# A linear-attention and feed-forward kernel on one Trainium2 core: one padded bf16 copy of v in place of two copies, and a new written order of the work

## The chip, the cores and the metric

The kernel runs on one core of one Trainium2 chip (trn2). The time is device microseconds (us) of one launch; the median of three runs of the kernel before is 179.17 us (178.84 to 181.43). All profiles show the one core. Engines are named as in the profile: PE is TensorE's matrix multiply and PEld its loading of weights, DVE is VectorE, ACT is ScalarE, POOL is GpSimd, SP is SyncE, which issues all DMAs here.

## The reference

A gated recurrence over time (4 batches, 8 heads, 768 steps, head size 48) is followed by a feed-forward layer over the 3072 tokens:

```
f = 1.0 / (1.0 + np.exp(-f_logit))
for t in range(S):
    state = f[:, :, t, :, None] * state + np.einsum('bhd,bhe->bhde', k[:, :, t], v[:, :, t])
    y[:, :, t] = np.einsum('bhd,bhde->bhe', q[:, :, t], state)
x = y.transpose(0, 2, 1, 3).reshape(B * S, H * D)      # 3072 x 384
h = x @ w_in                                           # 384 -> 2048
out = np.maximum(0.01 * h, h) @ w_out                  # 2048 -> 384
```

Inputs and output are fp32; the kernel's matrix products take bf16 operands and add up in fp32.

## The kernel before, in words

**Chunks and units.** Time is cut into six chunks of 128 steps. Within a chunk, the recurrence becomes matrix products: scores of k and q, masked to the lower triangle, times v, plus the state at the chunk's start times q. The work is cut into 12 units of 256 tokens. Units 0 to 3 ("paired") hold chunks 0 and 1 of one batch each; units 4 to 11 hold one chunk of two batches each. Words in the written order have the form name_unit_part, with the PSUM banks behind an @; a last number 0 or 1 picks an engine where there is a choice (for SBUF work 0 is DVE and 1 is POOL; where PSUM is read 0 is DVE and 1 is ACT).

**Steps of a unit.** The loads Lf, Lk, Lq, Lv (line 201 for paired units, 205 for others) bring 192 KB each. ACT works out log f (ge, gl; lines 233 and 245). PE sums it along time (cs, lines 254 to 265) with the constant matrices bu, bs and ut and the vector half_ones; ACT takes exponentials of the sums (dec, lines 273 to 279: em, at, end). DVE or POOL multiplies k and q with them (k, q, line 285). The products are turned: by PE and a copy out of PSUM for units 0 to 3 (tk, tq, line 319; ck, cq, lines 332 and 334), by a DMA that SP issues for the others (xk, xq, line 339). PE makes scores (sc, lines 355 and 362), DVE masks them (mk, lines 372 and 376; units 0 to 3 use the constant pair_mask, which eight small DVE copies of bu and bs build, Mp, line 139). PE multiplies masked scores with v (mx, line 393) and adds the state's part (within mx, and ms for paired units, the same line). DVE or ACT copies the result to xT (xt, lines 453 and 455). The state is carried by PE (pt, lines 466 and 471: k times v), DVE (sf, lines 481 and 483) and POOL (sb, lines 488 and 491).

**Feed-forward.** For each unit, eight up words (line 499) of six matmuls each multiply xT with w_in; ACT applies the leaky ReLU (pr, line 504); eight dn words (line 520) of four matmuls each, four for each half of the unit, multiply with w_out; DVE or ACT copies out (ob, lines 529 and 531) and SP stores (st, line 535). The very last half of unit 11 is done in two column halves (dc, oc, sh; lines 542 to 557). The weights arrive in fp32 (WI, WO, lines 154 and 158) and are cast by DVE, POOL or ACT (ci, co, lines 165 and 167); an up word of a group needs that group's ci.

**The copies of v.** mx multiplies in blocks of 32 output columns, three to a pair of heads (a pair has 2 x 48 = 96 columns). Blocks 0 and 2 lie within one head. Block 1 straddles: its first 16 columns are the end of head 0 and the next 16 the beginning of head 1, and each head's masked scores are multiplied separately, so each head needs 32 columns of which the other head's 16 are zero. So v is kept twice: vb holds v in bf16 (line 291), and v2 holds four groups of 16 columns a pair, the outer two copied from v (lines 297 and 300) and the inner two zero (cleared once, line 108). Paired units take three casts a half (one at line 291, two at 297), others two a unit (291 and 300).

**What sets the order.** The schedule is written out by hand: the string order (lines 576 to 642) is read word by word, and each engine gets its instructions in that order. Every engine runs its own queue strictly in order, and an instruction that waits holds up all behind it on that engine. SP's queue holds the loads, the DMA transposes and the stores. F words (line 97) are matmuls of zeros on PE whose result is not used. At the start the order holds the clearing of pads (Zl, Zk, Zq, Zv, lines 104 and 108), of the state buffers (Zb, line 111), and the building of constants on POOL (Mt: ut; Ms: bs; Mu: bu; both of the latter line 118; Mh: half_ones; Mi: ident).

## Time and profile before

| What | Value |
|---|---|
| Median of three runs | 179.17 us (178.84 to 181.43) |
| The profiled execution's own time | 178.92 us |
| Its span in the trace | 177.1 us, granted TensorE clock 0.999 |
| PE matmul busy | 170.0 us, 2308 instructions |
| PE weight loads busy | 124.9 us |
| DVE busy | 80.2 us |
| ACT busy | 108.8 us |
| POOL busy | 77.3 us |
| DMA | 34.45 MB, mean 194 GB/s |

The span is measured from the first to the last instruction of the program that the trace holds; the execution's own time is 1.8 us longer. The views used are: the page (shares of engines and of the chain that ended last), the windows (busy time of each engine in stretches of the span), the waits (who waited for whom), the chain in order of time, the timeline of an engine, and the groups of instructions by line and shape. In a timeline row stand the start, the length, the engine, the line, the operation, output<-inputs, shapes and count; a bracket at the end gives the idle time before it and what ended it.

### The profile page before, as it was taken

The numbers are of one execution on the slowest core, as the hardware profiler recorded it, in microseconds if no ns is written. First come the engines' busy times: TensorE is split into PE (matmuls) and PEld (weight loads), VectorE is DVE, ScalarE is ACT, GpSimd is POOL, SyncE is SP. The second block draws the span as 40 slices with busy tenths as digits, with TensorE's granted clock in tenths as the row PEclk, the third lists the DMA queues.
The fourth block names the chain that finished last, engine by engine and source line by source line (L and its number), as shares of the span: only waits on it lengthen the run. The fifth ranks groups of instructions, "written<-read, shape, count | busy, mean of one in ns | idle before, by whom it ended". The sixth has DMA issues, their size and how long they took to land.

```text
span 177.1 us, 5587 instructions
## 1 busy us (share of the span) xinstructions
PE 170.0 (96%) x2308; PEld 124.9 (71%) x2310; DVE 80.2 (45%) x170; ACT 108.8 (61%) x230; POOL 77.3 (44%) x141
## 2 busy tenths in 40 slices
...
GB/s 127 270 286 331 343 314 367 381 288 238 213 156 78 187 176 250 180 222 182 219 188 211 228 163 166 196 195 225 192 184 209 141 232 167 48 44 0 4 67 113
DMA packets 108330, 34.45 MB, mean 194 GB/s; under 512 B 101008, under 2 KB 107280, under 8 KB 108304
## 3 DMA queue, kind: packets, MB, share of 16 engines
...
q8 instruction: 18, 0.29, 0.7%
...
## 4 chain that ended last, share of the span: by engine, by line
PE 87%; DVE 4%; DMA 3%; ACT 2%; issue 2%; POOL 1%; SPq 1%; DVEq 0%; POOLq 0%
PE ps L520 34%; PE ps L499 34%; PE ps L393 6%; DMA f_raw<-in_f_logit_dram 3%; PE ps L362 2%; PE ps L319 2%; DVE wm L372 2%; PE ps L262 2%; PE ps L542 1%; PE ps L355 1%; PE ps L471 1%; PE ps L97 1%; DVE kh L285 1%; POOL sb L491 1%; DVE sf L481 1%
## 5 line engine op out<-in xcount | busy, mean ns | idle before, releaser
L504 ACT ACTIVATE gT<-ps 128x512 bf16<-128x512 f32 x96 | 53.1, 608 | 27.1 <-PE ps L499 26.7
L499 PE MATMUL ps<-xT,w_in 128*128 128x256 bf16 x576 | 69.6, 273 | 0.1
L520 PE MATMUL ps<-w_out,gT 128*128 128x384 bf16 x368 | 67.3, 326 | 0.0
L499 PEld LDWEIGHTS <-w_in 128*128 128x128 bf16 x576 | 55.1, 98 | 9.2 <-DVE xT L455 0.4
L520 PEld LDWEIGHTS <-gT 128*128 128x128 bf16 x368 | 34.4, 98 | 19.8
L285 POOL TENSOR_TENSOR qh<-q_raw,at 128x768 bf16<-128x768 f32 (+1 forms) x13 | 18.3, 1405 | 21.9 <-ACT end L279 7.3
L376 DVE TENSOR_TENSOR wm<-ps,ut 128x512 bf16<-128x512 f32 x32 | 20.1, 684 | 10.6 <-PE ps L362 10.6
L273 ACT ACTIVATE em<-ps 128x384 bf16<-128x384 f32 x24 | 11.9, 496 | 19.8 <-PE ps L265 9.3
L483 DVE TENSOR_TENSOR sf<-sf,ps 64x192 f32<-64x192 f32 x32 | 11.2, 349 | 18.0 <-PE ps L471 16.1
L491 POOL CAST sb<-sf 64x192 bf16<-64x192 f32 x40 | 14.5, 362 | 7.2 <-DVE sf L481 4.9
L285 POOL TENSOR_TENSOR kh<-k_raw,em 128x768 bf16<-128x768 f32 (+1 forms) x9 | 14.4, 1604 | 5.7 <-DMA q_raw<-in_q_dram 3.2
L291 POOL CAST vb<-v_raw 128x384 bf16<-128x384 f32 (+1 forms) x13 | 8.5, 650 | 16.7 <-DMA v_raw<-in_v_dram 13.3
L488 POOL TENSOR_TENSOR sf<-sf,end 128x192 f32<-128x192 f32 x16 | 8.9, 554 | 14.2 <-DVE sf L483 13.9
L531 DVE COPY osb<-ps 128x384 f32<-128x384 f32 x13 | 7.2, 554 | 16.1 <-PE ps L520 10.5
L233 ACT ACTIVATE e<-f_raw 128x384 f32<-128x384 f32 (+1 forms) x16 | 11.1, 695 | 2.3 <-DMA f_raw<-in_f_logit_dram 2.3
L274 ACT ACTIVATE at<-ps 128x384 bf16<-128x384 f32 x24 | 11.9, 497 | 0.0
L372 DVE TENSOR_TENSOR wm<-ps,pair_mask 128x512 bf16<-128x512 f32 x16 | 10.4, 687 | 3.3 <-PE ps L355 3.0
L245 ACT ACTIVATE lf<-e 128x384 bf16<-128x384 f32 (+1 forms) x16 | 10.9, 683 | 0.3
L455 DVE CAST xT<-ps 128x384 bf16<-128x384 f32 x11 | 6.1, 566 | 10.3 <-PE ps L393 10.0
L453 ACT CAST xT<-ps 128x384 bf16<-128x384 f32 x13 | 6.6, 527 | 5.3 <-PE ps L393 5.0
L529 ACT COPY osb<-ps 128x384 f32<-128x384 f32 x10 | 4.9, 493 | 6.9 <-PE ps L520 6.9
L97 PE MATMUL ps<-zeros 128*128 128x512 bf16 x20 | 7.8, 467 | 1.4 <-DVE zeros L93 1.2
...
## 6 DMA issues: line engine op xcount, KB each, us to landing
...
```

Source lines behind the costliest of these rows:

```text
L233: nc.scalar.activation(e[:, part], src[:, part], AF.Exp, scale=-1.0)
L245: nc.scalar.activation(dst, src, AF.Ln, bias=1.0)
L273: nc.scalar.activation(ems[j % 2][:, a], t[:, 0:H * D], AF.Exp, scale=1.0)
L274: nc.scalar.activation(ats[j % 2][:, a], t[:, 0:H * D], AF.Exp, scale=-1.0)
L285: eng.tensor_mul(heads(j, to[j % NR], a)[:, :, :, 0:D], raw_heads(j, x, a), decays(j, by, a))
L372: nc.vector.tensor_mul(w.rearrange("t (s p) n -> t s p n", s=2), src.rearrange("t (s p n) -> t s p n", s=2, p=2), pair_mask[:, :, None, :] ...
L376: nc.vector.tensor_mul(w, src.rearrange("t (p n) -> t p n", p=P2), ut[:, None, :].to_broadcast([128, P2, 128]))
L483: nc.vector.tensor_add(sf[rows], sf[rows], new)
L491: nc.gpsimd.tensor_copy(out=sb[rows, :, y * D:y * D + D], in_=sf[rows])
L499: nc.tensor.matmul(pm[:, i, :], w_in_of(ff, kk), xT_of(j)[:, kk].rearrange("t a s -> t (a s)"), start=(kk == 0), stop=(kk == NK - 1))
L504: nc.scalar.activation(gT_of(j)[:, 2 * g:2 * g + 2, :], pm, AF.Prelu, alpha=0.01)
L520: nc.tensor.matmul(po, gT_of(j)[:, ff, 128 * a:128 * a + 128], w_out_b[ff // 2][:, ff % 2, :], start=(ff == 0), stop=(ff == NF - 1))
```

## The change

Three things change.

First, v has one bf16 copy instead of two. vbs becomes a tile of 80 columns a head: 48 of v and 32 of padding. In a pair of heads the columns are head 0 (0 to 47), zeros (48 to 79), head 1 (80 to 127), and padding that nothing reads (128 to 159). Blocks 0 and 2 of a pair are columns 0 to 31 and 96 to 127; the straddling block's two parts are columns 32 to 63 (the end of head 0, then 16 zeros) and 64 to 95 (16 zeros, then the beginning of head 1). So cast_v is one cast a call in place of two or three, the tiles v2 are gone, clear_v clears columns 48 to 79 of each pair (as many elements as clear_v2 cleared), and mix and state read from the one tile.

Second, the written order is another one. It holds the same words the same number of times, except that the F words hold 25 matmuls of zeros in place of 22. Within it, engines change for some words: the v casts of units 0 to 3 go 3 to DVE and 5 to POOL (before 1 and 7), those of units 4 to 11 go 6 to DVE and 2 to POOL (before 2 and 6); the k products of units 0 to 3 go 5 and 3 (before 7 and 1); xt goes 16 to DVE and 8 to ACT (before 11 and 13); of the casts of w_out DVE has 3 and POOL 3 (before 5 and 1); five of the eight Zb, and Mi, stand in POOL's queue ahead of Mu, where none of them did.

Third, the banks of PSUM behind the @ are new too, as part of the order.

The diff, with the two orders up to ms_2 and the new one's end:

```diff
--- before.py
+++ after.py
@@ -66,8 +66,8 @@
     ems = tiles(2, [128, 2, H * D], BF16, "em")
     ats = tiles(2, [128, 2, H * D], BF16, "at")
     ends = tiles(4, [128, 2, P2], FP32, "end")
-    vbs = tiles(3, [128, 2, H, D], BF16, "vb")
-    v2s = tiles(3, [128, 2 * P2, 4, 16], BF16, "v2")
+    VW = D + 32
+    vbs = tiles(3, [128, 2, H, VW], BF16, "vb")
     kTs = tiles(2, [128, 2 * P2, 128], BF16, "kT")
     qTs = tiles(2, [128, 2 * P2, 128], BF16, "qT")
     wms = tiles(8, [128, 4, 128], BF16, "wm")
@@ -104,8 +104,12 @@
             engine(e).memset(ts[i][:, :, :, D:64], 0.0)
         return go
 
-    def clear_v2(i, e):
-        engine(e).memset(v2s[i][:, :, 1:3, :], 0.0)
+    def clear_v(i, e):
+        engine(e).memset(pairs_of_v(vbs[i])[:, :, D:VW], 0.0)
+
+    def pairs_of_v(t):
+
+        return t.rearrange("t a (p j) n -> t (a p) (j n)", j=2)
 
     def clear_state(b, i, e):
         engine(e).memset(sbs[b][i], 0.0)
@@ -286,20 +290,7 @@
         return go
 
     def cast_v(j, a, e):
-        vb, v2 = vbs[j % 3], v2s[j % 3]
-        eng = engine(e)
-        eng.tensor_copy(out=heads(j, vb, a), in_=raw_heads(j, "v", a))
-        if paired(j):
-            p = slice(0, P2) if a == 2 else slice(2 * a, 2 * a + 2)
-            src = by_pair(raw(j, "v")).rearrange("t (p j) s d -> t j s p d", j=2)
-            dst = v2.rearrange("t (s p) n e -> t n s p e", s=2)
-            for i in range(2):
-                eng.tensor_copy(out=dst[:, 3 * i, :, p], in_=src[:, i, :, p, 32 - 32 * i:48 - 32 * i])
-        else:
-            a2 = slice(a, a + 1) if a < 2 else slice(0, 2)
-            eng.tensor_copy(out=v2[:, P2 * a2.start:P2 * a2.stop, 0:4:3, :],
-                                  in_=raw(j, "v")[:, a2].rearrange("t a (p j) d -> t (a p) (j d)", j=2)[:, :, 32:64]
-                                  .rearrange("t p (j e) -> t p j e", j=2))
+        engine(e).tensor_copy(out=heads(j, vbs[j % 3], a)[:, :, :, 0:D], in_=raw_heads(j, "v", a))
 
     def turned(j, x):
         return (kTs if x == "k" else qTs)[j % 2]
@@ -398,7 +389,7 @@
 
         for i, b in enumerate(bank):
             st[j]["py", i] = b
-        vb, v2 = vbs[j % 3], v2s[j % 3]
+        vp = pairs_of_v(vbs[j % 3])
         jobs = []
         if paired(j):
             halves = range(2) if a == 2 else (a,)
@@ -413,10 +404,8 @@
                 for g, which, p, y in todo:
                     for i in range(2):
                         rows = slice(64 * i, 64 * i + 64)
-                        if which == "v":
-                            lhsT = vb[rows, s, 2 * p + y, 16 * y:16 * y + 32]
-                        else:
-                            lhsT = v2[rows, P2 * s + p, 2 * y:2 * y + 2, :]
+                        at = 96 * y if which == "v" else 32 + 32 * y
+                        lhsT = vp[rows, P2 * s + p, at:at + 32]
                         jobs.append((i, g, lhsT, wm_of(j, p // 2, y)[rows, 2 * s + p % 2, :]))
             accumulate(j, jobs, (0,) if a else ())
             return
@@ -427,9 +416,9 @@
         for i in range(2):
             for y in range(2):
                 for p in range(P2):
-                    jobs.append((i, 3 * p + 2 * y, vb[:, i, 2 * p + y, 16 * y:16 * y + 32], wm_of(j, i, y)[:, p, :]))
+                    jobs.append((i, 3 * p + 2 * y, vp[:, P2 * i + p, 96 * y:96 * y + 32], wm_of(j, i, y)[:, p, :]))
                 for p in range(P2):
-                    jobs.append((i, 3 * p + 1, v2[:, P2 * i + p, 2 * y:2 * y + 2, :], wm_of(j, i, y)[:, p, :]))
+                    jobs.append((i, 3 * p + 1, vp[:, P2 * i + p, 32 + 32 * y:64 + 32 * y], wm_of(j, i, y)[:, p, :]))
         accumulate(j, jobs, (0, 1))
 
     def mix_state(j):
@@ -464,12 +453,12 @@
                     for i in range(2):
                         rows = slice(64 * i, 64 * i + 64)
                         nc.tensor.matmul(banks[bank[i]][:, 96 * p:96 * p + 96], kh[rows, s, 2 * p:2 * p + 2, :],
-                                         vb[rows, s, 2 * p:2 * p + 2, :], start=(s == 0), stop=(s == 1))
+                                         vb[rows, s, 2 * p:2 * p + 2, 0:D], start=(s == 0), stop=(s == 1))
             return
         st[j]["pt", a] = bank[0]
         for p in range(P2):
             nc.tensor.matmul(banks[bank[0]][:, 96 * p:96 * p + 96], kh[:, a, 2 * p:2 * p + 2, :],
-                             vb[:, a, 2 * p:2 * p + 2, :], start=True, stop=True)
+                             vb[:, a, 2 * p:2 * p + 2, 0:D], start=True, stop=True)
 
     def state_add(j, a):
         sf = sfs[batch(j, a)]
@@ -565,7 +554,7 @@
         "dc": down_cols, "oc": out_cols, "sh": store_cols,
         "Lf": load("f"), "Lk": load("k"), "Lq": load("q"), "Lv": load("v"),
         "WI": load_w_in, "WO": load_w_out, "ci": cast_w(w_in_b, 0), "co": cast_w(w_out_b, 8),
-        "Zl": clear_pad(lfs), "Zk": clear_pad(khs), "Zq": clear_pad(qhs), "Zv": clear_v2, "Zb": clear_state,
+        "Zl": clear_pad(lfs), "Zk": clear_pad(khs), "Zq": clear_pad(qhs), "Zv": clear_v, "Zb": clear_state,
         "Mu": make_block(bu, mybir.AluOpType.is_gt), "Ms": make_block(bs, mybir.AluOpType.is_ge), "Mi": make_ident,
         "Mo": make_ones, "Mh": make_half_ones, "Mp": make_pair_mask, "Zz": clear_zeros, "F": fill, "Mt": make_ut,
     }
@@ -573,73 +562,73 @@
 
 
     order = """
-    Zz F_7_512@7 Lf_1_0 Mt Ms Zb_0_0_0 Zl_2_0 Zv_1_1 Lf_0_1 Zl_1_0 Zv_0_1 Zb_0_1_0 Zk_0_0 Zb_1_1_0 Lf_0_0 Zq_0_0
-    Zq_1_0 Lk_0_1 Mh Mu Mp_0 Zk_2_1 Lq_0_1 Zb_1_0_0 Zl_0_0 Lq_0_0 Lk_0_0 ge_1_0 Lk_1_0 Zk_1_1 gl_1_0 ge_0_1
-    Zb_3_0_1 Zq_2_1 Mo Lq_1_0 gl_0_1 Mi Lf_1_1 Lv_0_1 ge_0_0 gl_0_0 cs_1_0@0 Zb_2_0_0 Lv_0_0 cs_0_1@1 F_2_512@7
-    dec_0_1 cs_0_0@2 F_1_512@7 Lk_1_1 dec_0_0 k_0_1_0 tk_0_1@3 q_0_1_0 tq_0_1@4 F_1_512@2 Zb_2_1_1 Lq_1_1
-    k_0_0_0 dec_1_0 Lv_1_1 ck_0_1_1 Lv_1_0 cq_0_1_0 tk_0_0@5 F_1_512@4 q_1_0_0 q_0_0_1 tq_0_0@6 Zv_2_0 Lf_2_1
-    cq_0_0_1 WI_5 k_1_0_1 ck_0_0_0 sc_0_1@7.1 ge_1_1 Lf_2_0 tq_1_0@2 gl_1_1 mk_0_1_1 sc_0_0@4.0 mk_0_0_1
-    mk_0_0_0 cq_1_0_1 tk_1_0@3 cs_1_1@5 F_3_512@0 ck_1_0_0 sc_1_0@6.1 v_0_1_1 v_0_0_1 pt_0_2@0.2 F_1_512@3
-    mk_0_1_0 WI_1 WI_0 dec_1_1 Lq_2_1 k_1_1_0 tk_1_1@4 q_1_1_1 WI_2 sf_0_0 v_1_0_1 tq_1_1@3 cq_1_1_1 ge_2_1
-    gl_2_1 ck_1_1_0 Lk_2_1 mx_0_2@5.7 xt_0_0_1 sb_0_0 v_1_1_1 WI_4 sc_1_1@0.4 F_3_512@3 mk_1_0_1 ci_5_1 mk_1_1_1
-    ms_0 xt_0_1_1 cs_2_1@3 mk_1_0_0 Lq_2_0 pt_1_2@1.4 F_1_512@6 sf_1_0 sb_1_0 up_0_5@5 F_1_512@1 mk_1_1_0 Lk_2_0
-    mx_1_2@6.7 ge_2_0 gl_2_0 dec_2_1 pr_0_5 ms_1 cs_2_0@1 ci_1_0 xt_1_1_0 WI_3 Lv_2_0 WI_7 xt_1_0_1 up_0_1@0
-    ci_0_1 Lv_2_1 q_2_1_1 up_1_5@3 pr_1_5 Zb_3_1_1 up_0_0@7 up_1_1@5 ci_2_0 sf_0_1 tq_2_1@6 up_1_0@3 pr_0_1 WO_0
-    k_2_1_0 up_0_2@0 WO_1 dec_2_0 tk_2_1@2 pr_0_2 pr_0_0 ci_4_0 sb_0_1 pr_1_1 cq_2_1_0 k_2_0_0 up_1_2@1 q_2_0_1
-    pr_1_2 up_0_4@0 up_1_4@6 Lf_3_0 WI_6 sf_1_1 pr_1_4 ci_3_0 tq_2_0@7 sb_1_1 tk_2_0@5 F_1_512@4 cq_2_0_1
-    ck_2_0_0 up_1_3@1 WO_2 sc_2_0@4.6 Lk_3_0 ck_2_1_0 v_2_0_1 pr_1_0 WO_3 mk_2_0_1 ci_7_2 mk_2_0_0 sc_2_1@5.7
-    up_0_3@2 pr_0_3 WO_7 mk_2_1_1 v_2_1_1 pt_2_2@3.6 pr_1_3 up_0_7@4 Lf_3_1 mk_2_1_0 up_1_7@2 pr_0_7 sf_2_0
-    sb_2_0 co_0_2 pr_1_7 ge_3_0 co_1_0 mx_2_2@7.1 xt_2_0_0 ms_2 xt_2_1_1 dn_0_0_0@5 ci_6_1 dn_0_1_0@4 sf_2_1
...
+    Zz F_10_512@7 Lf_0_1 Lf_1_0 Lf_0_0 Lk_0_1 Lk_0_0 Zb_1_1_0 Lq_0_1 Zb_1_0_1 Mi Zq_2_0 Zl_1_1 Lq_0_0 Zv_2_0
+    Zk_2_0 Zq_0_0 Mt Lv_0_0 Ms Zq_1_1 Lv_0_1 Zv_0_0 Lq_1_0 Lf_1_1 Zb_2_1_1 Lk_1_0 Zb_3_1_1 Mh Zk_0_1 Lq_1_1
+    Zb_0_0_1 Zl_0_0 Lk_1_1 Zb_0_1_1 Mu Mp_0 Zk_1_1 Zb_2_0_1 Lf_2_1 ge_0_1 gl_0_1 Lv_1_1 ge_1_0 gl_1_0 cs_0_1@0
+    F_1_512@7 Lv_1_0 Zb_3_0_0 Lf_2_0 WI_5 WI_1 ge_0_0 gl_0_0 cs_0_0@1 WI_0 cs_1_0@2 dec_0_1 k_0_1_0 tk_0_1@3
+    F_1_512@7 WI_4 Zv_1_1 dec_0_0 k_0_0_0 q_0_0_0 q_0_1_1 tq_0_1@4 cq_0_1_0 dec_1_0 v_0_0_1 ck_0_1_0 tk_0_0@5
+    ck_0_0_1 Lk_2_0 Lq_2_1 tq_0_0@6 F_1_512@1 cq_0_0_0 WI_2 WI_3 v_0_1_1 pt_0_2@7.0 sf_0_0 sc_0_1@1.2 mk_0_1_1
+    sc_0_0@4.3 F_3_512@6 mk_0_0_1 mk_0_0_0 ge_1_1 gl_1_1 cs_1_1@5 dec_1_1 q_1_0_1 tq_1_0@6 cq_1_0_0 k_1_0_1
+    tk_1_0@7 F_5_512@2 ck_1_0_1 sc_1_0@2.3 Lq_2_0 Mo k_1_1_0 tk_1_1@4 q_1_1_1 tq_1_1@6 sb_0_0 mk_0_1_0
+    mx_0_2@5.7 ms_0 Zl_2_0 v_1_0_1 mk_1_0_1 mk_1_0_0 ck_1_1_1 cq_1_1_1 sc_1_1@1.4 mk_1_1_1 mk_1_1_0 xt_0_1_1
+    Lk_2_1 v_1_1_1 pt_1_2@3.6 F_4_512@2 mx_1_2@2.7 sf_1_0 ge_2_0 gl_2_0 cs_2_0@4 sb_1_0 xt_0_0_0 ge_2_1 gl_2_1
+    cs_2_1@1 dec_2_1 ci_5_1 sf_0_1 xt_1_0_1 up_0_5@3 ci_1_0 up_0_1@5 pr_0_1 pr_0_5 ci_0_0 up_0_0@0 pr_0_0 WI_7
+    WO_0 sb_0_1 ms_1 sf_1_1 WO_1 ci_4_0 up_0_4@1 pr_0_4 xt_1_1_0 up_1_5@2 up_1_1@6 up_1_4@5 Lv_2_1 Lv_2_0
+    dec_2_0 WI_6 pr_1_5 k_2_0_0 tk_2_0@3 pr_1_4 up_1_0@0 pr_1_0 ci_2_0 up_0_2@7 pr_0_2 q_2_0_0 ck_2_0_0 q_2_1_1
+    tq_2_1@1 cq_2_1_0 WO_2 up_1_2@4 tq_2_0@2 cq_2_0_1 pr_1_2 ci_3_1 WO_3 up_1_3@5 pr_1_3 k_2_1_1 tk_2_1@0
+    ck_2_1_0 co_0_2 Lf_4_1 Lf_4_0 WO_5 pr_1_1 up_0_3@7 pr_0_3 sc_2_0@3.1 mk_2_0_0 mk_2_0_1 Lf_3_0 Lf_3_1
+    sc_2_1@2.4 mk_2_1_1 mk_2_1_0 ci_7_1 up_1_7@0 up_0_7@5 pr_0_7 pr_1_7 v_2_1_0 co_1_1 dn_0_1_0@3 dn_1_0_0@6
+    dn_1_1_0@1 v_2_0_0 pt_2_2@7.4 sf_2_0 sb_1_1 WO_4 mx_2_2@5.2 WO_7 Lk_3_1 ci_6_2 up_1_6@0 sb_2_0 ms_2 xt_2_1_0
...
+    dc_11_1_0_2 dc_11_1_0_3 oc_11_1_0_1 sh_11_1_0
```

99 lines of the change are left out of this document (49 added, 50 removed).

## The prediction

> **What bounds the kernel now.** I read the page's shares first, then the windows, then PE's waits, then PE's chain.
>
> ```profile
> PE 170.0 (96%) x2308; PEld 124.9 (71%) x2310; DVE 80.2 (45%) x170; ACT 108.8 (61%) x230; POOL 77.3 (44%) x141
> ...
> PE 87%; DVE 4%; DMA 3%; ACT 2%; issue 2%; POOL 1%; SPq 1%; DVEq 0%; POOLq 0%
> ```
>
> The second line is the chain that ended last: 87% of the span is PE itself. The windows (span stretch, length, then busy us of PE, PEld, DVE, ACT, POOL, granted clock, DMA share, GB/s) say where the rest lies:
>
> ```profile
> 0.00:22.00 22.00, 18.64 (x354) 11.09 (x357) 17.40 (x44) 15.63 (x36) 15.21 (x47) 1.00 0.96 271
> 22.00:60.00 38.00, 37.69 (x503) 28.27 (x499) 21.93 (x46) 26.09 (x56) 17.12 (x31) 1.00 0.92 249
> 60.00:174.00 114.00, 113.72 (x1489) 85.57 (x1462) 40.88 (x81) 66.94 (x140) 45.00 (x65) 1.00 0.78 164
> 174.00:177.10 3.10, 0.00 (x0) 0.00 (x0) 0.00 (x0) 0.10 (x1) 0.00 (x0) 0.95 0.27 98
> ```
>
> From 22 us to 174 us PE is idle for 0.31 + 0.28 us in all. The last 3.1 us are the last copy and store. So three places remain where an order can win or lose: the first 22 us, in which PE has only 354 of its 2308 matmuls and DVE is the fullest engine after PE (17.40 of 22); the 0.6 us of holes; and new holes that the order might make in a stretch that has none. PE's own waits (us in total, times, longest), the chain's rows (start, length, what) and PE's timeline give the holes a name:
>
> ```profile
> PE ps L393 <- POOL sb L491: 0.3, 1, 0.3
> ...
> PE ps L97 <- issue: 0.2, 1, 0.2
> ```
>
> ```profile
> 22.09 2.64 PE ps L499 x24
> ...
> 33.50 0.68 POOL sb L491
> ...
> 173.78 0.32 ACT osb L550
> ```
>
> ```profile
> 33.72 0.23 PE L393 MATMUL ps<-qT,sb 128*32 128x128 bf16 x1
> 34.22 0.35 PE L393 MATMUL ps<-qT,sb 128*32 128x128 bf16 x11 [0.27 <-POOL sb L491]
> ```
>
> At 22.09 the dense stream begins: 24 matmuls in 2.64 us, so an up word is 0.66 us. The one later wait of PE that the list names is ms_2 for the state copy sb_2_0, which ends at 34.18; PE started nothing from 33.72 to 34.22. PE waited only 0.2 us for "issue" anywhere, which is what an instruction block that comes late would look like: an order that minds TensorE's blocks has next to nothing to win back there.
>
> **The change, part by part.** *The casts.* The groups by line and shape (busy us, mean ns of one | idle before):
>
> ```profile
> L291 POOL CAST vb<-v_raw 128x768 bf16<-128x768 f32 x6 | 4.9, 823 | 9.9 <-DMA v_raw<-in_v_dram 6.7 <-PE ps L265 3.2
> L297 POOL CAST v<-v_raw 128x64 bf16<-128x64 f32 x14 | 3.5, 280 | 0.0
> L291 POOL CAST vb<-v_raw 128x384 bf16<-128x384 f32 x7 | 3.5, 503 | 6.7 <-DMA v_raw<-in_v_dram 6.6
> L300 POOL CAST v<-v_raw 128x256 bf16<-128x256 f32 x6 | 2.4, 398 | 0.0
> ...
> L291 DVE CAST vb<-v_raw 128x768 bf16<-128x768 f32 x2 | 1.2, 618 | 2.8 <-DMA v_raw<-in_v_dram 2.8
> ...
> L291 DVE CAST vb<-v_raw 128x384 bf16<-128x384 f32 x1 | 0.3, 349 | 0.0
> ```
>
> POOL loses the small casts (3.5 + 2.4 us) and keeps 5 x 0.503 + 2 x 0.823 = 4.2 us of the 8.4; together 10.1 us fewer. DVE goes from 1.6 us of large casts to 3 x 0.349 + 6 x 0.618 = 4.8 us. The rows hold no cast into rows of 80 columns; it may cost as now (349 ns for 384 elements) or as much as a two-input product of that size (560 ns, row 7.82 below), so 4.8 to 8 us; I take 4.8, since the number of elements is what the rows follow. None of it is on PE's chain: POOL is idle 100 us of the span, DVE 97 us, and PE waits for no v in the list above. Value: 0, with a bound of 0.5 us for a cast on DVE that stands among the four masks of one unit (v_6 stands between the third and the fourth). If DVE's slack after 60 us (40.88 busy of 114) were gone, each such cast would cost its 0.62 us.
>
> *PE's own work.* The words are the same, so the matmuls are the same and their operands have the same shapes. The F words go from 22 to 25 matmuls, all ahead of the dense stream, where PE waits anyway: 0.
>
> *The constants.* Five state clears and the identity now stand ahead of bu on POOL. POOL's timeline at the start:
>
> ```profile
> 0.73 0.20 POOL masks.py:65 MEMSET ut<- 128x128 bf16 x1 [0.29 <-POOLq L662]
> ...
> 3.94 0.57 POOL L104 MEMSET kh<- 128x256 bf16 x2
> 4.44 0.43 POOL L111 MEMSET sb<- 128x384 bf16 x1
> 4.80 0.32 POOL L104 MEMSET qh<- 128x256 bf16 x1
> ...
> 5.63 0.45 POOL L111 MEMSET sb<- 128x384 bf16 x1
> ```
>
> bu was ready at 3.94. From 0.73 to 5.63 (4.90 us) POOL did ut, bs, half_ones, bu, the identity, five pads and one state buffer. The new queue up to bu has three pads instead of five (two take from 3.94 to 4.44, so 0.50 less) and five state buffers instead of one (4 x 0.36 more, from 4.44 to 4.80): bu is ready at about 0.73 + 4.90 - 0.50 + 1.44 = 6.6 us, 2.6 us later. What hides that is ACT:
>
> ```profile
> 4.59 0.32 PE L254 MATMUL ps<-lf,bu 128*128 128x192 bf16 x1 [0.24 <-ACT lf L245]
> ...
> 6.33 0.52 ACT L233 ACTIVATE e<-f_raw 128x384 f32<-128x384 f32 x1 [0.82 <-DMA f_raw<-in_f_logit_dram]
> ...
> 7.32 0.47 ACT L273 ACTIVATE em<-ps 128x384 bf16<-128x384 f32 x1
> ```
>
> The first sum on PE moves from 4.59 to 6.6, but in both orders ACT's first exponential of a sum stands behind the third gate (ge_0_0, gl_0_0), whose load lands at 6.3, so em comes at 7.3 either way. Were that cover gone, the delay would be 2.0 us. What is late next is pair_mask, eight DVE copies that wait for bu, and behind them on DVE the first k product (7.82 below).
>
> *The start, by DVE's queue.* The rows that price it:
>
> ```profile
> 7.82 0.56 DVE L285 TENSOR_TENSOR kh<-k_raw,em 128x384 bf16<-128x384 f32 x1 [1.02 <-ACT em L273]
> ...
> 11.02 2.10 DVE L372 TENSOR_TENSOR wm<-ps,pair_mask 128x512 bf16<-128x512 f32 x3
> 13.04 0.41 DVE L334 COPY kT<-ps 128x512 bf16<-128x512 bf16 x1
> ...
> 13.96 1.19 DVE L285 TENSOR_TENSOR kh<-k_raw,em 128x384 bf16<-128x384 f32 x1
> ...
> 19.02 0.74 DVE L481 TENSOR_TENSOR sf<-ps,end 64x192 f32<-64x192 f32 x2 [0.76 <-ACT e L233]
> ...
> 20.40 1.14 DVE L167 CAST w_in<-k_raw 128x768 bf16<-128x768 f32 x1
> ```
>
> ```profile
> 13.83 0.91 POOL L285 TENSOR_TENSOR qh<-q_raw,at 128x384 bf16<-128x384 f32 x1 [0.83 <-ACT end L276]
> ...
> 19.44 0.81 POOL L491 CAST sb<-sf 64x192 bf16<-64x192 f32 x2 [1.15 <-DVE sf L481]
> 20.31 0.82 POOL L167 CAST w_in<-f_raw 128x768 bf16<-128x768 f32 x1
> ```
>
> DVE's new queue, from em at 7.8 to the last mask of unit 1: k, k, q and later k_1_1 (4 x 0.56), four copies out of the turning (4 x 0.41), sf_0_0 (0.74), eight masks (8 x 0.70): 10.2 us, so mk_1_1_0 ends at 18.0 if DVE never waits. Then sf_1_0 to 18.75, on POOL sb_1_0 to 19.6 and behind it ci_5_1 to 20.4, and the first up word at 20.4; each of the next three up words needs a cast of w_in from DVE's queue (ci_1, ci_0, ci_4, with 2 x 0.74 of state and 0.57 of xt before and between). From 18.75: 0.57 + 0.74, then ci_1 and ci_0, 0.74, then ci_4. Other DVE casts of this shape took 0.56:
>
> ```profile
> L167 DVE CAST w_out<-q_raw 128x768 bf16<-128x768 f32 x2 | 1.1, 560 | 0.1
> ```
>
> With such casts the fourth up word ends at 23.1, with casts of 1.14 at 24.9. In the old order one up word stands ahead of 22.09 and three follow, so the fourth ends at 22.09 + 3 x 0.66 = 24.07, with the same other words behind it. So the start is worth -0.9 to +0.8; the middle is zero. DVE's queue can also meet POOL on the way: k_1_1 took 1.19 us at 13.96 instead of 0.56 while POOL ran its q product from 13.83 to 14.74, so a meeting costs up to 0.63, and the new order puts q_0_1 on POOL just as DVE starts k_0_1. I add half of one meeting: **+0.3** (bounds -0.9 and +1.4).
>
> [...]
>
> *The hole at ms_2.* In the new order the word up_1_6 (0.66 us) stands between mx_2 and ms_2, so sb_2_0 has that much longer; the hole from 33.72 to 34.22 goes: **-0.5**. What is late next is nothing on PE; dn words follow.
>
> *New holes.* Between mx and a unit's first up word PE needs other work for the copies xt:
>
> ```profile
> L455 DVE CAST xT<-ps 128x384 bf16<-128x384 f32 x11 | 6.1, 566 | 10.3 <-PE ps L393 10.0
> ```
>
> Units 5, 6, 8 and 11 now have both copies on DVE (2 x 0.57 = 1.13 and the wait for PSUM) behind two dn words or their like (1.3 us): tight, but covered. Bounds 0 and 4 x 0.25 = 1.0; I take **+0.1**.
>
> The loads are the same 96 of 192 KB and 16 of 384 KB from one queue; w_in's parts 5, 1, 0, 4 are 19th to 22nd in place of 18th, 20th, 21st, 25th, and PE waits for no load in the list above. The stores and DMA transposes stay behind the same producers. The tail (last dc, copy, store) is the same: 0.
>
> **Sum**, against the profiled execution's own 178.92: 178.92 + 0.3 - 0.5 + 0.1 = **178.8 us**. The median of the runs is 0.25 above that execution, which is within their spread, so nothing is added.
>
> **The rivals.**
>
> *A denser start* (22%). POOL and DVE do not meet, the casts of w_in run at 0.56, and xt has cover: 178.92 - 0.9 - 0.5 = 177.5; if ci_5 also gets ahead of sb_1_0's wait, the stream starts at about 19.6 and another 0.8 is gone: 176.7. For it: the queue sum of 10.2 us has no wait in it. Against: DVE had 17.40 busy of 22 before, and its casts took 1.14 beside POOL's.
>
> *DVE's queue starts late* (20%, slower). pair_mask waits for bu at 6.6. Its copies of bu alone took 2.5 us beside POOL's clears:
>
> ```profile
> L139 DVE COPY pair_mask<-bu 64x64 bf16<-64x64 bf16 x6 | 2.5, 447 | 1.2 <-POOL bu L118 1.1
> ```
>
> Then k_0_1 starts at 9.1 instead of 7.8 and all of DVE's queue is 1.3 later; one whole meeting adds 0.63: 178.92 + 1.3 + 0.63 - 0.5 + 0.1 = 180.5. It decides from the point where pair_mask ends after 7.8. Against: after bu POOL has only two clears left (0.6 us).
>
> [...]
>
> *Blocks come late* (8%). The new order packs mx_0, ms_0, sc_1, pt_1 and mx_1 into some 4 us, more instructions a microsecond than before, and a fetch lasts long:
>
> ```profile
> q8 instruction: 18, 0.29, 0.7%
> ```
>
> 0.7% of 16 engines' 177.1 us, over 18 fetches, is 1.1 us each; one exposed gives 179.9. Against: PE's 0.2 us of "issue" now. This is also the case that the change does not do what it says.
>
> **How the numbers follow.** The forecast holds 50% with 178.0 to 179.8 as its own range; the others 22, 20 and 8%. The range 176.4 to 181.2 takes in the denser start with its further gain and the late queue with another meeting. A difference over 2% (3.6 us), about what a measurement of this kernel can tell from no change, needs under 175.6 or over 182.8: both lie outside every case by about a microsecond, so 6% and 6% for what no case holds, and 88% for within.
>
> **What would show it.** Right: POOL busy about 71 us (10.1 us fewer casts of v, four more other instructions) and DVE about 82; the first sum on PE near 6.6 and em still near 7.4; the dense stream from 20 to 24.5 with the fourth up word near 24.1; no hole at ms_2; PE from 24 to 174 idle less than 1 us. Wrong: em later than 7.8, pair_mask ending after 8.5, PE holes of over 1 us behind v, xt or a load, or PE waits for "issue" of over 0.5.

## The result and the profile after

The changed kernel takes 180.26 us (median of 20 runs, 179.83 to 180.98), the kernel before 178.98 us on the same chip. The ratio is 1.0065, with a 95% interval of 1.0046 to 1.0084: slower by 1.2 us. The forecast was 178.8, 0.1 under the profiled execution of before. The time lies inside the range (176.4 to 181.2) and inside the 2% of no change, but on the other side of the time before, and outside the 178.0 to 179.8 that the forecast gave to its own case.

The page's shares and the chain that ended last, after:

```profile
PE 170.7 (96%) x2311; PEld 126.0 (71%) x2313; DVE 80.0 (45%) x168; ACT 108.4 (61%) x227; POOL 72.9 (41%) x122
...
PE 86%; DVE 7%; POOL 3%; issue 1%; ACT 0%; POOLq 0%; DVEq 0%
```

POOL is at 72.9 us in place of 77.3 (forecast 71) and DVE stands where it stood (forecast 82), so the casts did about what was forecast. But DVE and POOL now hold 10% of the chain where they held 5%. The windows say in which stretch (the columns are those of the windows of before):

```profile
0.00:22.00 22.00, 18.98 (x347) 12.18 (x350) 15.45 (x43) 14.56 (x34) 15.74 (x43) 1.00 0.97 275
22.00:60.00 38.00, 36.72 (x469) 27.33 (x467) 22.04 (x43) 25.94 (x55) 17.41 (x25) 1.00 0.91 247
60.00:174.00 114.00, 114.00 (x1490) 85.66 (x1488) 42.54 (x84) 67.55 (x139) 39.80 (x55) 1.00 0.78 164
174.00:178.40 4.40, 1.01 (x13) 0.78 (x10) 0.00 (x0) 0.36 (x2) 0.00 (x0) 0.90 0.21 73
```

Between 22 and 60 us PE is idle for 1.28 us (before: 0.31). From 60 to 174 us it shows none, and the span ends 1.3 us later (178.4 against 177.1). PE's own waits, after:

```profile
PE ps L310 <- DVE kh L289: 0.9, 2, 0.5
PE ps L258 <- POOL bu L122: 0.8, 1, 0.8
PE ps L488 <- DVE w_in L171: 0.7, 1, 0.7
PE ps L488 <- DVE sf L472: 0.3, 1, 0.3
```

The lines moved: L258 is the first sum, L310 a turning matmul, L346 the scores, L488 an up word, L509 a dn word, L289 the k and q products, L293 the cast of v, L171 the casts of w_in, L325 the copies out of the turning, L384 mx and ms, L455 pt, L472 the state sum sf. PE's timeline names the places:

```profile
6.48 0.34 PE L258 MATMUL ps<-lf,bu 128*128 128x192 bf16 x1 [0.84 <-POOL bu L122]
...
21.20 2.38 PE L488 MATMUL ps<-xT,w_in 128*128 128x256 bf16 x18 [0.33 <-DVE sf L472]
23.51 0.35 PE L384 MATMUL ps<-qT,sb 128*32 128x128 bf16 x12
24.59 2.14 PE L488 MATMUL ps<-xT,w_in 128*128 128x256 bf16 x18 [0.73 <-DVE w_in L171]
```

How to read the last three: 18 matmuls are three up words, 18 x 0.11 = 1.97 us of work. They hold PE from 21.20 to 23.51, so about 0.3 us of them is a stop in the middle (below: an instruction block). Then ms_1, and a stop of 0.73 for the fourth up word's w_in. (From here on a hole is the time between two starts less what the words between them take in the dense stream: 0.80 here, where the bracket, which goes by modelled ends, has 0.73.) The kernel before at this place, and a little later:

```profile
21.95 2.78 PE L499 MATMUL ps<-xT,w_in 128*128 128x256 bf16 x24
...
28.73 0.38 PE L97 MATMUL ps<-zeros 128*128 128x512 bf16 x1
```

The first row holds four up words, the second to the fifth (the first stands at 19.08), so the word behind the fourth starts at 21.95 + 18 x 0.109 = 23.91. In the changed kernel the word behind the fourth starts at 25.26, 1.35 us later, with the same words ahead of it. (The prediction's 24.07 counts from 22.09, the end of the matmul ahead of the row.)

To place every loss I compared the times at which the two traces had done the same work on PE, with the F words left out and each word priced at what it takes in the dense stream. The figures are good to about 0.1 us. Two of them need no prices, because both kernels have then done the same words: 1.35 after the fourth up word, and 1.27 at PE's end (175.01 against 173.74).

```
at (us):          22     25     34    35    50    53    60    170
after - before: +0.1  +1.35   +0.8  +0.3  +0.5  +1.1  +1.3   +1.3
```

So the start lost 1.35 us by 25 us; 1.0 came back by 35 us, most of it at places of before that the new order does not have (an F word inside the dense stream, 0.22 at 28.73, and 0.14 + 0.50 at ms_2); about 0.9 was lost again by 60 us, of which 0.63 is the hole at 51.8 us and 0.16 a wait of pt_3 at 54.4 us; nothing after that.

### The profile page after: what moved, and what is told of

The parts are those of the page before. It is cut to its first block, busy times and chain, and to the rows that moved or that the text cites. A ratio compares the mean times of both kernels' runs of the same rounds, so it can differ in the third digit from the quotient of the medians.

```text
span 178.4 us, 5556 instructions
## 1 busy us (share of the span) xinstructions
PE 170.7 (96%) x2311; PEld 126.0 (71%) x2313; DVE 80.0 (45%) x168; ACT 108.4 (61%) x227; POOL 72.9 (41%) x122
## 4 chain that ended last, share of the span: by engine, by line
PE 86%; DVE 7%; POOL 3%; issue 1%; ACT 0%; POOLq 0%; DVEq 0%
PE ps L488 35%; PE ps L509 33%; PE ps L384 6%; PE ps L353 2%; DVE wm L363 2%; PE ps L310 2%; PE ps L266 2%; PE ps L531 1%; DVE w_in L171 1%; PE ps L460 1%; DVE kh L289 1%; PE ps L258 1%; PE ps L346 1%; POOL sb L115 1%; DVE sf L472 1%
## 5 line engine op out<-in xcount | busy, mean ns | idle before, releaser
L493 ACT ACTIVATE gT<-ps 128x512 bf16<-128x512 f32 x96 | 54.2, 607 | 38.1 <-PE ps L488 37.3
L488 PE MATMUL ps<-xT,w_in 128*128 128x256 bf16 x576 | 70.2, 273 | 1.1 <-DVE w_in L171 0.7
L509 PE MATMUL ps<-w_out,gT 128*128 128x384 bf16 x368 | 66.2, 326 | 0.0
L488 PEld LDWEIGHTS <-w_in 128*128 128x128 bf16 x576 | 54.7, 98 | 10.6 <-DVE w_in L171 0.9
L509 PEld LDWEIGHTS <-gT 128*128 128x128 bf16 x368 | 34.8, 98 | 20.0
L289 POOL TENSOR_TENSOR kh<-k_raw,em 128x768 bf16<-128x768 f32 (+1 forms) x11 | 15.9, 1446 | 26.5 <-ACT em L277 19.2
L289 POOL TENSOR_TENSOR qh<-q_raw,at 128x768 bf16<-128x768 f32 (+1 forms) x13 | 17.8, 1372 | 8.5 <-PE ps L384 5.1
L520 DVE COPY osb<-ps 128x384 f32<-128x384 f32 x12 | 6.6, 555 | 24.5 <-PE ps L509 24.5
L472 DVE TENSOR_TENSOR sf<-sf,ps 64x192 f32<-64x192 f32 x32 | 11.2, 351 | 11.9 <-PE ps L460 11.1
L444 DVE CAST xT<-ps 128x384 bf16<-128x384 f32 x16 | 8.6, 563 | 14.4 <-PE ps L384 14.3
L97 PE MATMUL ps<-zeros 128*128 128x512 bf16 x23 | 8.9, 508 | 1.4 <-DVE zeros L93 1.2
L442 ACT CAST xT<-ps 128x384 bf16<-128x384 f32 x8 | 4.3, 545 | 8.0 <-PE ps L384 8.0
L293 POOL CAST vb<-v_raw 128x384 bf16<-128x384 f32 (+1 forms) x7 | 5.0, 736 | 9.3 <-DMA v_raw<-in_v_dram 9.2
L384 PE MATMUL ps<-wm,vb 64*32 64x128 bf16 (+1 forms) x512 | 8.4, 219 | 0.0
```

Of the source, the lines that this page charges most:

```text
L289: eng.tensor_mul(heads(j, to[j % NR], a)[:, :, :, 0:D], raw_heads(j, x, a), decays(j, by, a))
L384: nc.tensor.matmul(banks[st[j]["py", i]][32 * r:32 * r + 32, 128 * kk:128 * kk + 128], lhsT, rhs, start=(i, r) not in begun, stop=i in las ...
L472: nc.vector.tensor_add(sf[rows], sf[rows], new)
L488: nc.tensor.matmul(pm[:, i, :], w_in_of(ff, kk), xT_of(j)[:, kk].rearrange("t a s -> t (a s)"), start=(kk == 0), stop=(kk == NK - 1))
L493: nc.scalar.activation(gT_of(j)[:, 2 * g:2 * g + 2, :], pm, AF.Prelu, alpha=0.01)
L509: nc.tensor.matmul(po, gT_of(j)[:, ff, 128 * a:128 * a + 128], w_out_b[ff // 2][:, ff % 2, :], start=(ff == 0), stop=(ff == NF - 1))
```

## The experiments

The times below are medians, each with its ratio to the kernel before as it ran in the same job; that kernel's median was 178.8 to 179.3 us in these jobs.

**The two halves of the change.** e1_tile_old_order has the padded copy under the old order, e2_copies_new_order the two copies under the new one.

> The single padded copy of v with the old written order, so only the tile change. Theory (the order alone costs the 1.3 us; the casts are off PE's chain): within 0.3 us of the kernel before, POOL busy near 71 us (77.3 less the 5.9 us of small casts). Rival (the padded tile itself costs: slower casts into rows of 80, or slower reads of v by PE): 0.5 us or more above the kernel before, with casts at line 293 clearly longer than 503 ns for 384 elements on POOL.

Measured: 179.52 us, 1.0023 (1.0001 to 1.0044).

> The two copies of v with the new written order, so only the order change. [...] Rival (the padded tile costs): back within 0.3 us of the kernel before.

Measured: 184.08 us, 1.0270 (1.0235 to 1.0304). The two halves do not add. Under the old order the padded copy wins nothing, as forecast (an off-path cast is worth 0). Under the new order it wins 2.7% - 0.65% = 2.0%, 3.7 us. In e2's trace about half of this, 1.7 us, is lost near 54 us, where that order has put casts of v so that PE waits behind them; about 1 us more is lost near 151 us, where PE waits for a cast of v and then 0.58 us for a DMA transpose. The trace of e2 near 54 us (all engines in order of time; e2 has the line numbers of before: L285 the products, L291 and L297 the casts of v, L334 the copies out of the turning, L355 the scores):

```profile
53.92 0.97 DVE L291 CAST vb<-v_raw 128x384 bf16<-128x384 f32 x1
54.64 1.75 POOL L285 TENSOR_TENSOR qh<-q_raw,at 128x768 bf16<-128x768 f32 x1
...
54.81 1.73 DVE L297 CAST v<-v_raw 128x64 bf16<-128x64 f32 x2
...
56.46 0.41 DVE L334 COPY kT<-ps 128x512 bf16<-128x512 bf16 x1
...
56.93 0.64 PE L355 MATMUL ps<-qT,kT 48*64 48x128 bf16 x32 [1.46 <-DVE kT L334]
```

Two small casts take 1.73 us on DVE while POOL runs a product of 1.75; the copy of the turned k stands behind them, and PE's scores behind that copy.

**An earlier start.** e3_bu_first builds bu first on POOL; e4_more_fill has three more F matmuls, so that PE has work until the sums come.

```diff
-Zb_1_0_1 Mi Zq_2_0 ... Zb_0_1_1 Mu Mp_0
+Mu Zb_1_0_1 Mi Zq_2_0 ... Zb_0_1_1 Mp_0
```

> The changed kernel with bu built first on POOL, ahead of the five clears and the identity; nothing else moves. Theory A (the late bu sets the start: PE waited 0.84 us for it, em came at 7.42 where the third gate was done at 6.76, and PE was still at the slow clock till 9.9): em near 6.9, fourth up word 0.6 to 1.2 us earlier than 25.2, time 179.1 to 179.7. Theory B (the DVE queue and the chain sb_1, ci_5, ci_4 set the start, bu only shifts idle time): fourth up word within 0.3 of 25.2, time 180.0 to 180.4.

Measured: 180.78 us, 1.0095 (1.0065 to 1.0125). The first sum came at 5.43 in place of 6.48 and em at 6.39 in place of 7.42, yet PE stood 0.63 us inside up_0_1, 0.40 ahead of up_0_4 and 0.36 ahead of unit 2's turning, and no gain was left.

```diff
-Zz F_10_512@7
+Zz F_13_512@7
```

> The changed kernel with 13 matmuls of zeros at the start in place of 10, so that PE has work until bu is there at 6.4; nothing else moves. Theory of the clock (PE's idle stretch from 5.6 to 6.5 kept it slow, and the slow sums made em of unit 0 part 0 come at 8.6): sums at 82 ns for 192 columns from 7 us on, that em at 8.2 to 8.3, time 0.2 to 0.4 us lower. Rival (those steps have cover): the sums are faster and the time stays within 0.2 of the changed kernel's.

Measured: 180.96 us, 1.0099 (1.0073 to 1.0126). The sums ran at 82 ns each from 6.5 us (160 ns in the changed kernel, until 9.9), and the second em came at 7.89 in place of 8.60. That the slow pace is one of TensorE's clock I infer from two readings: at a granted clock of 0.50 matmuls took twice their time (f1 below, 0.32 in place of 0.16 us), and a trace's records of the granted clock begin where the pace doubles (at 10.27 us in the changed kernel, at 6.12 in the one before). The windows, with 1.00 for the first 22 us of each, do not show it. Again nothing was won: the hole ahead of up_0_4 grew to 0.91. What limits the stretch at 20 to 25 us is not the beginning of the chain.

**The places themselves.** f1_turn3 covers the late product k_3_1 with two dn words; f2_ci4_act takes the late cast of w_in to ACT; f3_casts_early puts four casts of w_in where each can run as soon as its load has landed; f4_both is f1 and f3.

```diff
 f1: -tk_3_1@0 tq_3_0@6 cq_3_0_0 dn_0_1_2 dn_0_1_3 v_3_0_0
     +dn_0_1_2 dn_0_1_3 tk_3_1@0 tq_3_0@6 cq_3_0_0 v_3_0_0
 f2: -xt_1_0_1 up_0_5@3 ... WO_1 ci_4_0 up_0_4@1
     +xt_1_0_1 ci_4_2 up_0_5@3 ... WO_1 up_0_4@1
 f3: f2, and
     -cs_2_0@4 sb_1_0 ... cs_2_1@1 dec_2_1 ci_5_1 sf_0_1 ... ci_1_0 up_0_1@5 pr_0_1 pr_0_5 ci_0_0 up_0_0@0
     +cs_2_0@4 ci_5_1 sb_1_0 ... cs_2_1@1 ci_0_2 dec_2_1 ci_1_0 sf_0_1 ... up_0_1@5 pr_0_1 pr_0_5 up_0_0@0
```

> The changed kernel with two dn words moved ahead of the word that turns k_3_1, so that k_3_1's late product has 0.65 us more cover. Theory A (what the changed kernel lost stands in PE's single holes, and none is given back later): the hole of 0.63 us near 51.8 us goes and the time falls by 0.5 to 0.6 us, to about 179.7. Theory B (a hole that is closed opens elsewhere, since PE then runs ahead of the casts and loads): another hole appears by 60 us and the time stays within 0.2 us of the changed kernel.

Measured: 183.39 us, 1.0213 (1.0171 to 1.0255): by the ratios 2.6 us worse than the changed kernel, which neither theory had. The hole did go from 51.8, and came back larger. First the changed kernel at that place, then f1:

```profile
50.37 0.92 POOL L289 TENSOR_TENSOR qh<-q_raw,at 128x384 bf16<-128x384 f32 x1 [0.49 <-DMA k_raw<-in_k_dram]
...
50.63 1.06 DVE L289 TENSOR_TENSOR qh<-q_raw,at 128x384 bf16<-128x384 f32 x1
...
51.23 0.83 POOL L293 CAST vb<-v_raw 128x384 bf16<-128x384 f32 x1
...
51.62 0.85 DVE L289 TENSOR_TENSOR kh<-k_raw,em 128x384 bf16<-128x384 f32 x1
...
52.53 0.40 PE L310 MATMUL ps<-ident,kh 128*128 128x128 bf16 x4 [0.47 <-DVE kh L289]
```

```profile
54.16 1.63 POOL L289 TENSOR_TENSOR qh<-q_raw,at 128x768 bf16<-128x768 f32 x1
...
54.29 1.72 DVE L293 CAST vb<-v_raw 128x384 bf16<-128x384 f32 x1
...
56.06 0.52 PE L455 MATMUL ps<-vb,kh 64*128 64x96 bf16 x16 [2.21 <-DVE vb L293]
...
57.08 3.66 PE L509 MATMUL ps<-w_out,gT 128*128 128x384 bf16 x12
```

In the first fence DVE's two products take 1.06 and 0.85 us where they take 0.56 alone: POOL's instructions end at 51.29 and 52.06, DVE's at 51.69 and 52.47, each about 0.4 us after the one that it met. In the second fence the cast of v, 0.35 us alone and 0.79 in the changed kernel, takes 1.72: it began 0.13 us behind POOL's long q product and ended 0.22 after it (54.16 + 1.63 = 55.79 for POOL's end, 56.01 for the cast's). In the changed kernel the two dn words stood between the turning and pt_3 and covered it; f1 had taken that cover away. And the hole had a tail: nine matmuls behind it, from 57.65 to 60.5 us, stand 0.32 us apart where dn matmuls stand 0.16 apart elsewhere, another 1.4 us; the granted clock of that stretch, 57.49 to 60.90, was 0.50.

> The changed kernel with one cast of w_in (part 4) moved from DVE, where it took 1.20 us behind a state sum, to ACT behind xt_1_0. Theory A: the hole of 0.80 us ahead of up_0_4 shrinks to 0.2 or less and the time falls by 0.5 to 0.8 us. Theory B (the loads and the instruction block are what set the start): the hole moves to up_0_1 or to the next unit's first words and the time stays within 0.2 us of the changed kernel.

Measured: 179.86 us, 1.0054 (1.0033 to 1.0076). The hole of 0.80 ahead of up_0_4 went, but the stop inside up_0_1 was 1.11 us in place of 0.24:

```profile
23.37 1.03 PE L488 MATMUL ps<-xT,w_in 128*128 128x256 bf16 x8 [0.94 <-issue]
```

> The changed kernel with four casts of w_in placed so that each runs as soon as its load has landed: part 5 ahead of the state copy sb_1_0 on POOL (which stood idle 2.15 us there), part 1 ahead of sf_0_1 on DVE, parts 0 and 4 on ACT. Theory A: up_0_5 starts near 20.5 instead of 21.2, the fourth up word ends near 23.5 to 24.0 instead of 25.25, and the time falls by 1.2 to 1.7 us, to 178.6 to 179.1. Theory B: the dense stream starts earlier but meets a wait for an instruction block (0.5 to 1.5 us, marked issue) or for the loads of unit 2, and the time falls by less than 0.5 us.

Measured: 180.50 us, 1.0061 (1.0030 to 1.0092), with runs from 179.0 to 181.1. In the trace the mend works: up_0_5 starts at 20.70 in place of 21.20, and PE has lost 0.9 us less by 25 us than in the changed kernel. The profiled execution, 179.43 us, is one of the short ones; the median shows no gain. Something that differs from run to run seems to take it back.

> f3_casts_early and f1_turn3 together. Theory A: the two gains add, 1.8 to 2.3 us, to 178.0 to 178.5, which would be faster than the kernel before. Theory B: no more than 0.5 us is won, and PE's holes of the start come again at the block or ahead of unit 2's words.

Measured: 182.67 us, 1.0206 (1.0168 to 1.0245), with f1's hole of 2.2 us and a stop of 1.11 inside up_0_1.

**The late instruction block.** "issue" is PE waiting for nothing that the profile shows. Where the stretch from 20 us on has such a stop, it stands at the same count in every trace, ahead of the 353rd weight load (the 352nd in e3 and i1, which build bu first), whatever word that load belongs to. The page has a queue q8 named "instruction" with 18 packets (16 KB each in the trace), below called fetches, and what one brings a block. Over PE's 2311 matmuls and 2313 weight loads after, that is one for 257 instructions; that q8 brings PE's is read from these counts and from the stops. The records of the second fetch of that queue, against that weight load, in eight of the 20 traces (us; gap: from the start of the load ahead, 0.02 to 0.11 where nothing stops):

```
kernel                 fetch starts   load 353 starts   between   gap
before                     19.54           21.84          2.31    0.08
after                      20.17           22.55          2.38    0.35
e1_tile_old_order          20.49           22.86          2.36    1.55
f1_turn3                   19.74           22.02          2.29    0.18
f2_ci4_act                 20.74           23.37          2.63    1.21
f3_casts_early             19.86           22.28          2.41    0.59
f4_both                    20.18           22.58          2.39    1.22
h3_all_full_fill           21.40           23.88          2.48    2.19
```

In none of the 20 traces did the load come sooner than 2.29 us after that fetch began. The fetch itself began anywhere from 19.4 to 21.4 us, beside loads that keep the DMA engines full (share 0.97 in the first 22 us). That this is what differs from run to run of one kernel is likely but not shown, since each kernel has one trace. The next stop ahead of this one stands at the 225th weight load (g4 below), 128 loads earlier, with 127 matmuls between the two in the trace of before and 130 in that of the changed kernel; so I count a block as 256 instructions, an estimate from these counts. To test this reading I moved the boundary by leaving out F matmuls, whose products are not used: g1_early_less_fill is f3 with 15 fewer, g2_less_fill the changed kernel with 15 fewer, g4_old_less_fill the kernel before with 10 fewer and with one dn word ahead of ms_2. g3_early_less_fill_v3 is g1 with another mend for the place at 52 us: one dn word ahead of the turning, one behind it, and v_3_0 cast on ACT.

```diff
 less fill: -F_10_512@7 ... F_3_512@6 ... F_5_512@2 ... F_4_512@2
            +F_1_512@7  ... F_1_512@6 ... F_3_512@2 ... F_2_512@2
 v3:        -tk_3_1@0 tq_3_0@6 cq_3_0_0 dn_0_1_2 dn_0_1_3 v_3_0_0 v_3_1_1
            +dn_0_1_2 tk_3_1@0 tq_3_0@6 v_3_0_2 cq_3_0_0 dn_0_1_3 v_3_1_1
 g4:        -xt_2_0_0 ms_2 xt_2_1_1 dn_0_0_0@5
            +xt_2_0_0 dn_0_0_0@5 ms_2 xt_2_1_1
```

> f3_casts_early with 15 of the 25 F matmuls left out (10 at the start become 1, and 3, 5 and 4 become 1, 3 and 2), so that the 256-instruction block which PE waited for in ten traces is entered 15 weight loads later in the words, inside up_0_4 rather than up_0_1. Theory A (the early casts were worth 1.2 to 1.7 us and a late block took them back: the first matmul behind the block stood 2.29 to 2.63 us after that block's fetch began, in all ten traces): no wait marked issue over 0.3 us after 15 us, median 178.8 to 179.2. Theory B (the fill matmuls keep TensorE's clock up, the block is minor): the sums of the start run at 160 ns for longer, PE's stream starts later, and the time is 180.5 or more.

Measured: 179.72 us, 1.0041 (1.0020 to 1.0063), eleven of its twelve runs within 179.3 and 180.0. The stop inside up_0_1 is gone and the runs lie closer together than f3's; the median is above the 178.8 to 179.2 that theory A had, and against f3 the ratio falls by 0.002, which the intervals do not tell from nothing.

> The changed kernel with 15 of its 25 F matmuls left out, as in g1_early_less_fill, and nothing else. Theory A: the hole of 0.24 us inside up_0_1 goes, those ahead of up_0_5 and up_0_4 (0.46 and 0.80 us) stay: 179.7 to 180.1. Theory B: slower by more than 0.3 us, at 180.6 or more, by a slower clock at the start.

Measured: 180.48 us, 1.0066 (1.0043 to 1.0090), as the changed kernel. Its stop of 0.24 went, its other holes stayed (0.46 and 0.95), and with fewer F words DVE's masks opened one of 0.52 inside mx_1. Its trace also waits 0.56 us at 149 us for a DMA transpose and 0.80 at 155 us for a cast of v; the changed kernel's trace has neither.

> The kernel before with 10 of its F matmuls left out (the 7 at the start become 1, two groups of 3 become 1) and one dn word put ahead of ms_2, where PE stood 0.50 us. Theory A: the block is entered 10 weight loads later and no longer meets its fetch, and the hole at ms_2 goes: 0.5 to 1.0 us faster than the kernel before. Theory B: the hole moves behind ms_2 or the start's clock falls, and the time stays within 0.2 us of the kernel before.

Measured: 179.84 us, 1.0034 (1.0009 to 1.0059), a miss for both theories. The hole at ms_2 is gone and the 353rd load has no stop, but the boundary one block ahead, at the 225th weight load, had moved into ms_0:

```profile
18.06 0.29 PE L393 MATMUL ps<-qT,sb 128*32 128x128 bf16 x6 [0.25 <-POOL vb L291]
19.26 0.29 PE L393 MATMUL ps<-qT,sb 128*32 128x128 bf16 x6 [0.91 <-issue]
```

ms_0 stops in its middle for no operand, and goes on 2.31 us after the first fetch of q8 began (16.95).

> g1_early_less_fill with one dn word put ahead of the word that turns k_3_1, and the cast of v_3_0 on ACT instead of DVE. Theory A (f1_turn3 lost 2.2 us because this one cast took 1.72 us on DVE beside POOL's q product and the sums pt_3 waited for it, and then PE ran at half speed): no hole over 0.2 us from 49 to 60 us and 0.5 to 0.6 us less than g1_early_less_fill. Theory B (the copies of the turned k and q on DVE are the limit there): a hole of 0.4 us or more ahead of pt_3 or sc_3_1, and no gain.

Measured: 178.64 us, 0.9980 (0.9959 to 1.0002). The place at 52 us has no hole now. The ratio is 0.0061 below g1's, where 0.5 to 0.6 us (0.003) had been expected; the two intervals do not meet, so this place is shown to be a part of the loss. The difference, 1.1 us, is more than the hole of 0.63, and why is open.

```profile
51.59 0.81 PE L509 MATMUL ps<-w_out,gT 128*128 128x384 bf16 x4
52.24 0.39 PE L310 MATMUL ps<-ident,kh 128*128 128x128 bf16 x4
52.47 0.39 PE L310 MATMUL ps<-ident,qh 128*128 128x128 bf16 x4
52.69 0.81 PE L509 MATMUL ps<-w_out,gT 128*128 128x384 bf16 x4
53.43 0.52 PE L455 MATMUL ps<-vb,kh 64*128 64x96 bf16 x16
```

**One place at a time, and all together.** h1_v3 is the changed kernel with the v3 edit alone. h2_all is g3 with dn_9_0_2 moved ahead of sc_11_2, which in several traces of the new order waited 0.1 to 0.6 us for a DMA transpose. h3_all_full_fill is h2_all with all 25 F matmuls. h4_old_ms2 is the kernel before with the one dn word ahead of ms_2.

> The changed kernel with one dn word ahead of the word that turns k_3_1 and the cast of v_3_0 on ACT instead of DVE, and nothing else. Theory A (the loss at 51.8 us is a place of its own, where one cast of v on DVE meets POOL's products): 0.6 to 1.1 us under the changed kernel, ratio to the kernel before near 1.002. Theory B (the loss of the start swallows or hides it): ratio of 1.005 or more, as for the changed kernel.

Measured: 179.74 us, 1.0040 (1.0017 to 1.0062): by the ratios 0.45 us under the changed kernel, where 0.6 to 1.1 had been expected, with intervals that overlap.

> g3_early_less_fill_v3 with the word dn_9_0_2 put between mx_10 and sc_11, where PE waited 0.1 to 0.6 us for the turned q of unit 11 in five traces of the new order. Theory A (that wait is a third place of the new order's loss): 0.2 to 0.4 us under g3_early_less_fill_v3, ratio near 0.996. Theory B (the late wait is a store or load queue's and moves on with the words): no change.

Measured: 178.96 us, 1.0000 (0.9980 to 1.0021): no gain over g3 that these runs can tell, so the wait at unit 11 is not shown to be a part of the loss.

> The same as h2_all with all 25 F matmuls kept. Theory A (the block that is late behind the loads costs the start 0.3 to 1.2 us): 0.5 to 1.0 us slower than h2_all, with runs that spread over 1.5 us or more and a wait marked issue inside up_0_1. Theory B (the F matmuls are worth their place): equal to h2_all or faster.

Measured: 179.28 us, 1.0013 (0.9991 to 1.0036): 0.1 to 0.2% above h2_all, less than expected and within the intervals, so a cost of the block in the median is not shown. Against the changed kernel (1.0046 to 1.0084) the intervals do not meet: with the same F words, the early casts, v3 and dn_9_0_2 together take the loss back. Its profiled execution, at 181.97 us far above that median, shows what a late block can cost:

```profile
20.82 1.14 PE L488 MATMUL ps<-xT,w_in 128*128 128x256 bf16 x9
23.87 1.44 PE L488 MATMUL ps<-xT,w_in 128*128 128x256 bf16 x6 [1.92 <-issue]
```

The six matmuls behind that stop take 1.44 us, the nine ahead of it 1.14: half the pace (granted clock 0.50 from 23.88 to 27.30).

> The kernel before with one dn word put ahead of ms_2 and nothing else: the one gain that was forecast for the new order, alone. Theory A (the hole was PE's only one there): 0.4 to 0.6 us faster than the kernel before. Theory B (what PE wins there it waits for later): within 0.2 us of it.

Measured: 178.53 us, 0.9985 (0.9963 to 1.0006). The hole is gone in its trace; by the medians it was worth 0.54 us, but the interval reaches no gain.

> h2_all with bu first on POOL, so that the first sum on PE comes at 5.4 us instead of 6.5. Theory A (with the early casts, the block moved and the meeting at 52 us gone, nothing is left to take an earlier start back, as it was in e3_bu_first): 0.4 to 0.8 us under h2_all, ratio near 0.996, faster than both kernels. Theory B (from 18 us on the start waits for the weight loads, and the wave of loads is the same): within 0.2 us of h2_all, ratio near 1.000.

Measured: 178.56 us, 0.9969 (0.9948 to 0.9989). With every place mended, the new order is faster than both kernels, than the one before by 0.3%. It is not told apart from the old order with its one hole mended (h4 above, i2 below). That bu first is what made the difference to h2_all is not shown: the two intervals overlap, and at 25 us the two traces stand 0.5 us apart the other way.

> One padded copy of v, the old order, and one dn word put ahead of ms_2: the two parts of the change that could win, without the new order. Theory A (the order alone brought the loss): no slower than the kernel before, ratio 0.997 to 1.000. Theory B (the casts of the padded copy cost something of their own): 1.002 or more, as for the padded copy under the old order.

Measured: 179.14 us, 0.9987 (0.9967 to 1.0008): as h4_old_ms2, so the padded copy is free to about 0.2%, and the loss came with the order. e1, at 1.0023, leaves room for a small cost, but its casts one by one take what they took before (349 ns for 384 elements on DVE in both kernels, 822 and 823 for 768 on POOL).

## Why the prediction was wrong, point by point

- **The casts, 0: right.** POOL 72.9 (forecast 71), DVE 80.0 (82), 4.7 us of DVE's casts (4.8); under the old order the padded copy costs nothing that these runs can tell (i2 beside h4). The bound of 0.5 us was given to a cast among four masks; the cast that stood at the edge was v_3_0, ahead of pt_3 (0.16).
- **PE's own work, 0: wrong by 0.2.** The F words do not all stand ahead of the dense stream: one of before's stands at 28.73 and takes 0.22 us there, and the new order has none at that place.
- **The constants, 0: right in its time, short in its reach.** The first sum came at 6.48 (6.6 forecast), em at 7.42 (7.3). It also kept the sums at half pace (160 ns each, against 82 in e4), and DVE stood 0.62 us for the second em (e4, with the sums at full pace, has that em 0.71 us earlier). That was not the cause of the loss by itself: bu first (e3) and the sums at full pace (e4) gave nothing.
- **The start, +0.3 with bounds -0.9 and +1.4: the step that failed.** It measured +1.35 at the fourth up word, at the upper bound: the places were the right ones, the size was not. Two parts of the sum were too small. The sum of DVE's queue, 10.2 us to the last mask, had "no wait in it", and mk_1_1_0 ended at 19.1 instead of 18.0. The term for meetings allowed half of one meeting of DVE and POOL. DVE's timeline has two waits (0.62 for the second em, 0.29 for PE's scores) and two meetings in that queue, a q product of 0.85 us and a k product of 1.04 instead of 0.56:

```profile
9.12 0.58 DVE L289 TENSOR_TENSOR kh<-k_raw,em 128x384 bf16<-128x384 f32 x1 [0.62 <-ACT em L277]
9.62 0.85 DVE L289 TENSOR_TENSOR qh<-q_raw,at 128x384 bf16<-128x384 f32 x1
...
14.63 1.04 DVE L289 TENSOR_TENSOR kh<-k_raw,em 128x384 bf16<-128x384 f32 x1
...
17.84 1.29 DVE L363 TENSOR_TENSOR wm<-ps,pair_mask 128x512 bf16<-128x512 f32 x2 [0.29 <-PE ps L346]
```

  Behind the masks, the three casts of w_in took 0.56, 0.86 and 1.20 us, the last one beside a product of POOL:

```profile
23.21 0.91 POOL L289 TENSOR_TENSOR qh<-q_raw,at 128x384 bf16<-128x384 f32 x1
23.34 1.20 DVE L171 CAST w_in<-f_raw 128x768 bf16<-128x768 f32 x1
```

  The working gave 23.1 for the fourth up word with casts of 0.56 and 24.9 with casts of 1.14, and took a value between. It was through at 25.26, which is about 23.1, plus 1.1 for the late masks and 0.9 for the casts: the cast that PE waited for directly was the one that met POOL's product. The other two stops, of 0.24 at the 353rd load and 0.46 ahead of the first up word, cost nothing on top: DVE's queue had no gap over 0.05 us from 19.04 to 24.54, and the fourth up word waits for its end.
- **New holes, +0.1: the second failure.** I priced the xt copies (unit 7 has both on DVE too); none of them made a hole of that size. The hole came at a place that I had not looked at, 0.63 us ahead of tk_3_1, from two meetings in 2 us. The v3 edit takes it away: g3 is 0.0061 below g1, h1 0.0025 below the changed kernel.
- **ms_2, -0.5: right**, 0.64 by the holes of the trace, 0.54 by the medians of h4, though h4's interval reaches 1.
- **The rivals.** "DVE's queue starts late" named the time (180.5) and the engine, but its condition did not hold: pair_mask ended at 7.28 and em came on time, so the queue did not start late; it was slowed on the way, and that the rival's figure came out near the measured time is luck. "Blocks come late" had its evidence against it in one line, 0.2 us of "issue" in one execution of before. That row stands at the 225th load and says little of the 353rd: there the same order stopped 1.45 us in e1's profiled execution:

```profile
22.86 0.15 PEld L263 LDWEIGHTS <-lf 128*128 128x128 bf16 x3 [1.45 <-issue]
```

- **The signs.** None of those that were to show the forecast wrong came: em 7.42, pair_mask 7.28, holes of at most 0.80, "issue" of 0.24. Of those that were to show it right, the fourth up word near 24.1 failed. The bounds were wide enough to hide a loss made of pieces of 0.2 to 0.8 us.

What the runs account for: early casts and v3 together, with the wait at unit 11 moved, take the ratio from 1.0065 to 1.0013 (h3), fewer F matmuls to 1.0000 (h2). Each alone moves it less: f3 to 1.0061, h1 to 1.0040, g2 not at all. The intervals, each about 0.002 to 0.003 to either side, allow that these parts simply add. That the start's share is DVE's queue and its casts is read from the traces and from h3 as a whole; the early casts alone (f3) did not show it in the median. What stays open is how much of the 1.2 us is the block in a typical run: the traces show stops from nothing to 2.1 us, but only one execution of each kernel has a trace, and h3 beside h2, 0.1 to 0.2% apart, is within the intervals.
